# Linear attention and MLP on one core: scores and states per 64 tokens from block 1 on, with another order of the work

## The chip, the core and the metric

The kernel runs on one core of one Trainium2 chip. A core has TensorE (PE, matrix products; its weight loads are listed apart as PEld), VectorE (DVE), ScalarE (ACT), GpSimd (POOL) and SyncE (SP), which here only issues transfers. The engines run side by side and wait for one another through semaphores. On-chip memory is SBUF; PE writes into PSUM, which has eight banks. The metric is device time in microseconds (us), lower is better.

## What is computed

Inputs are x (4, 8, 768, 32), decays a (4, 8, 768), B and C (4, 8, 768, 16), and an MLP with g_ln (256), w_ch1 (256 x 1024) and w_ch2 (1024 x 256), all float32. Cut to what matters:

```python
# per batch and head; chunk = 32, state starts at 0
cum = np.cumsum(np.log(np.clip(a, 1e-06, 1.0)), axis=-1)          # within the chunk
M = einsum('in,jn->ij', C, B) * exp(cum_i - cum_j) * causal
y[chunk] = M @ x + (C @ state) * exp(cum_i)
state = exp(cum_last) * state + sum_j exp(cum_last - cum_j) * B_j x_j
# then per token, over the 8 x 32 = 256 features of all heads:
xn = (y - mean(y)) / sqrt(var(y) + 1e-06) * g_ln
out = y + relu(xn @ w_ch1) @ w_ch2
```

The result does not depend on the chunk length except by rounding, so a kernel may carry the state over other stretches.

## The kernel before, in words

The 768 tokens are 6 blocks t of 128. Within a block, tokens are cut into halves of 64 (HALF, index j), the partitions 0 to 63 and 64 to 127 of a tile; the four batches are split in NU = 2 (u) by NV = 2 (v), and heads are paired (q, four pairs; g, two groups of four heads). The steps, by the name that the order at the end of the file gives them:

- Head: the constants (`ld early`, on the ACT queue) and the decays (`ld a`, SP) are loaded; logarithms (`l1`, `l2`), sums and their exponentials (`e`, `x`, `so`, `sm`, `mb`, `sp`, `em`) give decay tables; two scans on DVE (`u`, `d`) give the decays since the start of a sub-chunk of 32 and to its end. For block 0 a product spreads these over all rows (`U`, `ur`); for later blocks they go out to memory and come back broadcast (`ro`, `ld ud`).
- `C`, `cm`, `B`: scaled C (split by even and odd head) and scaled B. `ones`, `W`: the mask tiles WW (two, one for each u), filled with the causal mask and then, for each block, with decays (three copies for each u, line 162).
- `G t u` (line 381): scores of one u, 128 tokens against 128. Keys of the first half meet all 128 queries (256 columns), keys of the second half only theirs (128 columns). `R t u q` (line 388, DVE): scores times mask.
- `I t` (line 400): queries of 128 tokens times the carried state; `V t u` (line 415): R times x, added in the same PSUM tile; `Z t` (line 427): what the block adds to the state, in a third part of the same PSUM tiles. `K`, `S`, `sb` (lines 432, 441, 445): the old state decayed, the new state, and its copy with a head mask, which I of the next block reads. So the state is carried once per 128 tokens, and Z of a block stands behind its I.
- The weights come in as 64-bit words and are put together (`k0`, `k2`, `k3`, `kr`, `f`), centred (`gd`, `wc`, `wm`, `ws`) and split in an upper and a lower part (`wh`, `wl`).
- The MLP: `y`, `yh`, `yl` copy and split y; `T`, `tw`, `tc` turn it to token order through memory; `st`, `ag`, `rs`, `rc` are its statistics. `h t m` (line 510): six products for one eighth of the hidden layer, in block 0 for each u apart (256 columns), later for all 512; `hh` (ACT) and `hl` (DVE) empty its bank. `o t b` (lines 537, 538) is the output of one batch, `oe` adds the residual, `od` stores it.

The order is written out in one string (ISSUE) of such names with an engine letter; each engine works through its own instructions in that order, and the transfers of SP are one queue in that order too. PSUM is one pool of eight banks, each taken by one tile at a time. `fill` products keep PE busy at the start. A product of float32 operands is two matmuls in the trace, one of float32r operands is one.

## Time and profile before

| | before |
|---|---|
| median of 3 runs | 190.06 us (190.02 to 193.27) |
| the profiled execution | 190.03 us |
| its span, first to last instruction | 188.3 us |
| PE busy | 181.6 us (96%), 2440 matmuls |
| DVE, ACT, POOL busy | 134.5, 72.9, 51.6 us |
| mean granted TensorE clock | 0.997 of full speed |

Busy time is the time in which at least one instruction of the engine runs. A row of the timeline is: start, time, engine, line, operation, out<-in, count, and in brackets the idle time of the engine just before it and what ended that. Matmuls overlap, so what one costs is read from the start of a group to the start of the next. A q behind an engine's name (SPq) means its sequencer.

### The profile page before, as it was taken

Reading aid. Unit: us, or ns where it says so; the run is one execution under the profiler, and the core shown is the slowest. Engines: PE = TensorE matmul, PEld = TensorE weight load, DVE = VectorE, ACT = ScalarE, POOL = GpSimd, SP = SyncE. Lnnn points to the kernel's source line nnn. Section 1 sums busy time; section 2 is a strip of 40 time slices with the busy share of each in tenths; the row PEclk is TensorE's granted clock in tenths of the full one; section 3 lists DMA queues with packets and bytes.
Section 4 is the critical chain, followed back from the end, with each engine's and each line's share of the span. In section 5 each row is a group of like instructions: output and inputs, shape, how many; then the busy total and the mean of one; then the engine's idle time right before and its main releaser. Section 6 shows DMA issues by size and latency. Waiting matters only on the chain.

```text
span 188.3 us, 5714 instructions
## 1 busy us (share of the span) xinstructions
PE 181.6 (96%) x2440; PEld 148.6 (79%) x2440; DVE 134.5 (71%) x302; ACT 72.9 (39%) x148; POOL 51.6 (27%) x65
## 2 busy tenths in 40 slices
PE   8979999999999999999998999999999999999992
PEld 8655589987878778788776887888888888888892
DVE  4899999998986797776984846659607574545841
ACT  7799999719434124421341201233102330034100
POOL 3162646624978941230032530000002000000000
PEclk9999999999999999999999999999999999999998
DMA  5999993843883913572150000363001035100102
GB/s 188 410 370 251 334 376 139 216 136 93 292 285 97 215 42 139 173 252 88 44 151 7 3 0 28 109 193 91 3 0 56 31 141 139 35 20 3 56 28 84
DMA packets 16729, 25.04 MB, mean 133 GB/s; under 512 B 4160, under 2 KB 10688, under 8 KB 16704
## 3 DMA queue, kind: packets, MB, share of 16 engines
q1 hardware_dynamic: 16560, 24.45, 40.3%
q8 instruction: 19, 0.31, 0.7%
q10 hardware_dynamic: 144, 0.23, 0.3%
q14 instruction: 6, 0.05, 0.1%
HBM read 18.06 MB, written 6.62 MB: 131 GB/s over the span
## 4 chain that ended last, share of the span: by engine, by line
PE 92%; ACT 4%; DVE 1%; issue 1%
PE ph L510 37%; PE po L537 23%; PE po L538 12%; PE yps L415 6%; PE G L381 4%; PE idle L556 2%; PE yps L427 2%; PE yps L400 2%; DVE R L388 1%; PE wc L226 1%; PE po L534 1%; ACT WW L162 1%; PE wc L227 1%; ACT raw L207 1%; ACT yh L162 1%
## 5 line engine op out<-in xcount | busy, mean ns | idle before, releaser
L537 PE MATMUL po<-w,hh 128*128 128x512 f32 x184 | 64.9, 396 | 0.1
L516 ACT ACTIVATE hh<-ph 128x512 fp32r<-128x512 f32 (+1 forms) x56 | 28.3, 536 | 74.0 <-PE ph L510 48.9
L510 PE MATMUL ph<-yh,w 128*128 128x512 f32 (+1 forms) x224 | 54.6, 365 | 0.0
L538 PE MATMUL po<-w,hl 128*128 128x256 f32 x184 | 47.9, 281 | 0.0
L522 DVE SCALAR_TENSOR_TENSOR hl<-ph,hh 128x512 fp32r<-128x512 f32 (+1 forms) x56 | 32.2, 604 | 17.1 <-ACT hh L516 17.1
L510 PEld LDWEIGHTS ph<-yh,w 128*128 128x128 f32 x224 | 38.2, 189 | 7.1 <-issue 0.3
L537 PEld LDWEIGHTS po<-w,hh 128*128 128x128 f32 x184 | 33.7, 188 | 7.1 <-ACT y L162 0.4
L538 PEld LDWEIGHTS po<-w,hl 128*128 128x128 f32 x184 | 34.7, 188 | 1.7
L510 PE MATMUL ph<-yl,w 128*128 128x512 f32 (+1 forms) x112 | 31.2, 360 | 0.0
L388 DVE TENSOR_TENSOR R<-G,WW 128x384 f32<-128x384 f32 x48 | 24.6, 546 | 5.6 <-PE G L381 4.9
L547 DVE SCALAR_TENSOR_TENSOR o<-po,rstd,ytok 128x256 f32<-128x256 f32 x24 | 11.5, 477 | 21.2 <-PE po L537 19.1
L510 PEld LDWEIGHTS ph<-yl,w 128*128 128x128 f32 x112 | 20.0, 189 | 3.5
L162 POOL COPY WW<-wt 32x512 f32<-32x512 f32 (+1 forms) x15 | 10.4, 695 | 17.0 <-DVE R L388 16.4
L162 POOL CAST yh<-y 128x512 fp32r<-128x512 f32 x5 | 3.3, 676 | 40.9 <-PE ph L510 33.5
L381 PE MATMUL G<-cm,bs 32*64 32x256 f32 (+1 forms) x384 | 12.0, 335 | 1.7 <-DVE bs L351 1.0
L162 ACT COPY WW<-wt 32x512 f32<-32x512 f32 (+1 forms) x21 | 12.8, 614 | 0.9 <-DVE rstd L501 0.7
L381 PEld LDWEIGHTS G<-cm,bs 32*64 32x64 f32 x384 | 7.4, 131 | 6.0 <-issue 2.4
L212 POOL TENSOR_TENSOR top<-top,raw 128x512 int32<-128x512 int32 x6 | 8.1, 1361 | 14.3 <-ACT WW L162 4.5
L547 DVE SCALAR_TENSOR_TENSOR o<-po,rstd,o 128x256 f32<-128x256 f32 x23 | 11.1, 484 | 0.8
L415 PEld LDWEIGHTS yps<-R,xt 64*32 64x32 f32 x768 | 10.1, 105 | 2.0 <-issue 1.2
L415 PE MATMUL yps<-R,xt 64*32 64x64 f32 (+1 forms) x768 | 11.2, 249 | 0.0
L490 DVE BATCH_NORM_STATS2 st<-ytok 128x6 f32<-128x256 f32 x24 | 9.4, 415 | 0.0
(100 smaller groups left out, 178.2 us busy)
## 6 DMA issues: line engine op xcount, KB each, us to landing
raw<-in_w_dram SPq DMA_DIRECT2D x8, 512.0 KB, 6.1
xt<-in_x_dram SPq DMA_DIRECT2D x6, 512.0 KB, 6.0
scr<-yx SPq DMA_DIRECT2D x6, 512.0 KB, 2.9
ytok<-scr SPq DMA_DIRECT2D x24, 128.0 KB, 3.0
out_dram<-o SPq DMA_DIRECT2D x24, 128.0 KB, 1.7
ud<-scr SPq DMA_DIRECT2D x10, 256.0 KB, 4.0
c<-in_cn_dram SPq DMA_DIRECT2D x6, 256.0 KB, 4.7
b<-in_bn_dram SPq DMA_DIRECT2D x6, 256.0 KB, 3.9
```

Source lines behind the costliest of these rows:

```text
L162: (e.copy if e is nc.scalar else e.tensor_copy)(dst, src)
L212: e.tensor_tensor(out=f, in0=f, in1=words.pop((w, *at))[0], op=ALU.add)
L381: nc.tensor.matmul(G[q][HALF * v:HALF * (v + 1), :, at], bs[r, i0 + HALF * j:i0 + HALF * (j + 1)], cm[r, :, i0 + HALF * j:i0 + P], start=T ...
L388: nc.vector.tensor_tensor(out=flat(R), in0=flat(tiles.pop(("G", t, u, q))), in1=flat(WW[u][:, 2 * q:2 * q + 2]), op=ALU.mult)
L415: nc.tensor.matmul(tiles["y", t, v, g][c:c + 32, u, HALF * j:], x[p, (j * NU + u) * NH + h], tiles["R", t, u, h // 2][p, h % 2, at], start ...
L490: nc.vector.bn_stats(out=st, in_=tiles["ytok", t][:, :, b])
L510: nc.tensor.matmul(ph, W1[m // 4, k][:, s, mc], v[:, k, tok], start=(i == 0), stop=(i == len(cmb) - 1))
L516: nc.scalar.activation(tiles["hh", t, m][:, tok], tiles["ph", t, m, u], AF.Relu)
L522: nc.vector.scalar_tensor_tensor(out=tiles["hl", t, m][:, tok], in0=tiles.pop(("ph", t, m, u)), scalar=0.0, in1=tiles["hh", t, m][:, tok]. ...
L537: both = lambda: nc.tensor.matmul(po, hh, w[:, :, at], start=(m == 0), stop=last, skip_group_check=True)
L538: low = lambda: nc.tensor.matmul(po[:, 0], hl, w[:, 0, at], start=False, stop=False, skip_group_check=True)
L547: nc.vector.scalar_tensor_tensor(out=parts(o), in0=parts(po[:, i]), scalar=tiles["rstd", t][:, b], in1=rest, op0=ALU.mult, op1=ALU.add)
```

## The change

- From block 1 on the scores of a block are two squares of 64 by 64 tokens instead of the triangle of 128: `G t` is one step for both u, every product has 128 columns, and its result is one full bank for each q. The masks for it are one tile WC, filled by `on` (two copies of the causal mask) and `W t` (two copies per block). `R t q` is then four products of 512 columns instead of eight of 384. Block 0 stays as it was.
- The state is carried per 64 tokens: `I t` reads the state before the block for the first half and the state in its middle for the second half, 64 columns each; `Z t` stands ahead of it, has two banks of its own and is kept apart by half; `K t j`, `S t j` and `sb t j` are done for both halves. Block 5 now needs Z for its first half.
- `V t` has two parts by head group g instead of by u, all products with 64 columns, and the parts may stand apart.
- The sums and tables have seven coefficient blocks instead of six and `rg` builds four row groups, so that `ur` is four products of 128 columns instead of one of 512.
- Some constants share buffers (early, ends, own_ini), the pool of R has 8 buffers instead of 12, and the last block's bt is half loaded.
- The order (ISSUE) is new throughout. On SP, a and the first w1 piece are followed by the other three w1 pieces, then by the late constants, c and b.

Core of the diff, without the tables and the order:

```diff
-    def score(t, u):
+    def score(t, u=None):
 
         bs, cm = tiles["bs", t], tiles["cm", t]
+        if t:
+            G = [banks.tile([P, NU, 2, P], F32, tag="bank", name=f"G{t}{q}") for q in range(NQ)]
+            for j in range(2):
+                for u in range(NU):
+                    for q in range(NQ):
+                        r = slice(2 * DS * q, 2 * DS * (q + 1))
+                        for v in range(NV):
+                            at = slice((v * NU + u) * P + HALF * j, (v * NU + u) * P + HALF * (j + 1))
+                            nc.tensor.matmul(G[q][HALF * v:HALF * (v + 1), u, :, HALF * j:HALF * (j + 1)], bs[r, at], cm[r, :, at], start=True, stop=True)
+            for q in range(NQ):
+                tiles["G", t, q] = G[q]
+            return
...
-                    nc.tensor.matmul(tiles["y", t, v, q // 2][f, u], tiles["sbd", t - 1][r, b], c2[r, b * P:(b + 1) * P], start=(u == 0), stop=False, skip_group_check=True)
+        summed(t)
+        for j in range(2):
+            state = tiles["sbd", t, 0] if j else tiles["sbd", t - 1, 1]
...
+                        nc.tensor.matmul(tiles["y", t, v, q // 2][f, u, HALF * j:HALF * (j + 1)], state[r, b], c2[r, b * P + HALF * j:b * P + HALF * (j + 1)],
+                                         start=(u == j == 0), stop=False, skip_group_check=True)
...
-        Z = tiles["Z", t] = [tiles["y", t, v, 0][:, NU] for v in range(NV)]
+        Z = tiles["Z", t] = [banks.tile([P, 2, P], F32, tag="bank", name=f"Z{t}{v}") for v in range(NV)]
         for u in range(NU):
-            for j in range(2):
+            for j in range(1 if t == NT - 1 else 2):
...
-    def kept(t, e=nc.vector):
-        S = tiles["K", t] = p1.tile([P, NB, 2 * HD], F32, tag="K", name=f"K{t}")
-        e.tensor_tensor(out=S, in0=tiles["S", t - 1], in1=emt[:, t].unsqueeze(2).to_broadcast([P, NB, 2 * HD]), op=ALU.mult)
+    def kept(t, j, e=nc.vector):
+        K = tiles["K", t, j] = p1.tile([P, NB, 2 * HD], F32, tag="K", name=f"K{t}{j}")
+        e.tensor_tensor(out=K, in0=tiles["S", t, 0] if j else tiles["S", t - 1, 1], in1=emt[:, t, j].unsqueeze(2).to_broadcast([P, NB, 2 * HD]), op=ALU.mult)
```

What this does to the order on the engines, at three places. First PE, the scores of block 1, before (G are the four score tiles, ph a hidden tile of block 0, emps the spread of the decays):

```order
L510 MATMUL ph_503<-yl_394,w_287 128x256
L381 MATMUL G_517<-cm_478,bs_501 64x2x128 x2
L381 MATMUL G_518<-cm_478,bs_501 64x2x128 x2
L381 MATMUL G_519<-cm_478,bs_501 64x2x128 x2
L381 MATMUL G_520<-cm_478,bs_501 64x2x128 x2
L381 MATMUL G_517<-cm_478,bs_501 64x2x64 x2
L381 MATMUL G_518<-cm_478,bs_501 64x2x64 x2
L381 MATMUL G_519<-cm_478,bs_501 64x2x64 x2
L381 MATMUL G_520<-cm_478,bs_501 64x2x64 x2
L296 MATMUL emps<-mblk,cst 128x120
L510 MATMUL ph_546<-yh_393,w_396 128x256
```

and with the change (the last of its four rounds of G, and the first rows of Z, the block's addition to the state):

```order
L409 MATMUL G_544<-cm_501,bs_526 64x2x64 x2
L409 MATMUL G_545<-cm_501,bs_526 64x2x64 x2
L409 MATMUL G_546<-cm_501,bs_526 64x2x64 x2
L409 MATMUL G_547<-cm_501,bs_526 64x2x64 x2
L483 MATMUL Z_592<-xt_585,be_358 32x64
L483 MATMUL Z_593<-xt_585,be_358 32x64
```

One u with wide and narrow products became four equal rounds for both u, and Z follows at once, where before the hidden layer went on.

Second PE, where I of block 1 meets V, before:

```order
L400 MATMUL yps_775<-c_763,sbd_733 64x128
L400 MATMUL yps_777<-c_763,sbd_733 64x128
L415 MATMUL yps_774<-R_702,xt_499 32x128
L415 MATMUL yps_776<-R_702,xt_499 32x128
L415 MATMUL yps_774<-R_702,xt_499 32x128
```

and with the change:

```order
L451 MATMUL yps_718<-c_689,sbd_699 64x64
L451 MATMUL yps_720<-c_689,sbd_699 64x64
L468 MATMUL yps_717<-R_583,xt_585 32x64
L468 MATMUL yps_719<-R_583,xt_585 32x64
L468 MATMUL yps_717<-R_583,xt_585 32x64
```

I and V stand as before, with 64 columns each; sbd_699 is the state in the middle of block 1.

Third ACT, from its start (WW and WC are mask tiles, cst constants and logarithms, cfr coefficients, top and raw weight words, wt decays), before:

```order
L162 COPY WW_89<-causal 128x1536
L162 CAST cfr<-cst 128x384
L263 ACTIVATE cst<-cst 128x192
L162 COPY uds<-uds 128x160
L193 ACTIVATE top_142<-raw_137 128x512
L277 ACTIVATE wt<-ew 128x384
L207 ACTIVATE raw_137<-raw_137 128x512
```

and with the change:

```order
L169 COPY WC<-early 128x1024 x2
L169 COPY WW_88<-early 128x1536
L273 ACTIVATE cst<-cst 128x192
L203 ACTIVATE top_132<-raw_130 128x512
L169 CAST cfr<-cst 128x448
L217 ACTIVATE raw_130<-raw_130 128x512
L169 COPY uds<-uds 128x160
```

Two more mask copies stand ahead of the logarithm (cst<-cst), and weight work stands ahead of the coefficients and of the scan's copy (uds).

## Rows read from the trace of the kernel before

**Rows 1.** The page's first part: busy time, share of the span and instructions

```profile
PE 181.6 (96%) x2440; PEld 148.6 (79%) x2440; DVE 134.5 (71%) x302; ACT 72.9 (39%) x148; POOL 51.6 (27%) x65
```

**Rows 2.** Timeline of PE, block 2's scores and block 1's addition to the state

```profile
45.27 0.91 PE L381 MATMUL G<-cm,bs 32*64 32x256 f32 x32
46.10 0.86 PE L427 MATMUL yps<-xt,be 64*32 64x64 f32 x64
46.96 0.50 PE L537 MATMUL po<-w,hh 128*128 128x512 f32 x1
47.29 0.28 PE L538 MATMUL po<-w,hl 128*128 128x256 f32 x1
47.41 0.39 PE L537 MATMUL po<-w,hh 128*128 128x512 f32 x1
47.65 0.28 PE L538 MATMUL po<-w,hl 128*128 128x256 f32 x1
```

**Rows 3.** Timeline of PE, I and V of block 1

```profile
39.90 0.70 PE L400 MATMUL yps<-c,sbd 32*64 32x128 f32 x32
40.54 1.82 PE L415 MATMUL yps<-R,xt 64*32 64x128 f32 x128
42.29 0.50 PE L537 MATMUL po<-w,hh 128*128 128x512 f32 x1
```

**Rows 4.** Timeline of PE's weight loads (PEld), V of block 1

```profile
40.54 1.66 PEld L415 LDWEIGHTS yps<-R,xt 64*32 64x32 f32 x128 [0.17 <-issue]
```

**Rows 5.** Timeline of PE, block 4: I, and G interrupted

```profile
98.19 0.69 PE L400 MATMUL yps<-c,sbd 32*64 32x128 f32 x32
...
100.42 0.65 PE L381 MATMUL G<-cm,bs 32*64 32x256 f32 x4
101.81 0.90 PE L381 MATMUL G<-cm,bs 32*64 32x256 f32 x28 [0.74 <-issue]
```

**Rows 6.** The chain that ended last: start, us, what; hidden products

```profile
31.04 5.95 PE ph L510 x48
...
117.25 12.48 PE ph L510 x54
```

**Rows 7.** Timeline of all engines at the start: ACT's idle time

```profile
2.16 1.47 ACT L162 COPY WW<-causal 128x1536 f32<-128x1536 f32 x1
...
3.91 0.51 ACT L162 CAST cfr<-cst 128x384 f32<-128x384 uint8 x1 [0.28 <-DMA cst<-in_consts_dram]
...
...
5.04 0.33 ACT L162 COPY uds<-uds 128x160 f32<-128x160 f32 x1 [0.35 <-DVE uds L308]
...
6.61 0.49 ACT L277 ACTIVATE wt<-ew 128x384 f32<-128x384 f32 x1 [0.67 <-PE ew L274]
...
9.44 3.66 ACT L162 COPY WW<-wt 32x512 f32<-32x512 f32 x6
...
19.17 0.37 ACT L162 CAST yh<-yps 128x256 fp32r<-128x256 f32 x1
```

**Rows 8.** Timeline of PE: Z of block 0, the first hidden product, the spread

```profile
21.47 1.12 PE L427 MATMUL yps<-xt,be 64*32 64x64 f32 x64 [0.25 <-ACT yh L162]
22.52 0.74 PE L510 MATMUL ph<-yh,w 128*128 128x256 f32 x4
...
26.70 0.45 PE L296 MATMUL emps<-mblk,cst 32*128 32x120 f32 x2
```

**Rows 9.** The page's fifth part: what empties a hidden tile

```profile
L516 ACT ACTIVATE hh<-ph 128x512 fp32r<-128x512 f32 (+1 forms) x56 | 28.3, 536 | 74.0 <-PE ph L510 48.9
...
L522 DVE SCALAR_TENSOR_TENSOR hl<-ph,hh 128x512 fp32r<-128x512 f32 (+1 forms) x56 | 32.2, 604 | 17.1 <-ACT hh L516 17.1
```

**Rows 10.** Instructions on tile S: duration ns min/median/max, first and last start

```profile
L441 DVE TENSOR_TENSOR S<-yps,K x8: 254/281/291, 47.5 to 105.1; 128x128 f32<-128x128 f32 x8
L445 POOL TENSOR_TENSOR sbd<-S,cst x4: 633/637/642, 36.4 to 109.4; 128x256 f32<-128x256 f32 x4
```

**Rows 11.** Stretches: us, each engine's busy time, PEclk, DMA share, GB/s

```profile
4.00:5.00 1.00, 1.00 (x6) 1.00 (x6) 0.89 (x3) 0.69 (x2) 0.00 (x0) 1.00 1.02 399
```

## The prediction, made before the change was run

> **What bounds the kernel now.** I read the page's busy times first: TensorE is busy 181.6 of 188.3 us, every other engine far less [rows 1]. A busy TensorE need not be at its peak, so the next view is its timeline, read from the start of one group to the start of the next. An MLP output tile alternates a 512-column and a 256-column product, 0.24 us and 0.12 us apart [rows 2]; the hidden products run at 5.95/48 = 0.124 us (256 columns) and 12.48/54 = 0.231 us (512 columns) [rows 6]. These paces hold from the first hidden product at 22.52 us [rows 8] to the end: 16 half tiles x 6 x 0.124, 40 full tiles x 6 x 0.231, 23 output tiles x 8 x 0.36 and some 3 us for the last one make about 137 us, the attention groups of blocks 1 to 5 (below) about 27, and 22.5 + 137 + 27 is 186.5 of 188.3. So there is almost no slack behind 22.5 us. The change is worth what it takes out of TensorE's own sequence, plus what it does to the first 22.5 us.

> **Prices.** The trace counts two matmuls for each fp32 product, and so do I. One G group (16 of 256 and 16 of 128 columns) takes 45.27 to 46.10, 0.83 us; one Z (64 of 64 columns) 46.10 to 46.96, 0.86 [rows 2]; one I (32 of 128) 39.90 to 40.54, 0.64; one V (64 of 128 and 64 of 64) 40.54 to 42.29, 1.75 [rows 3]. Each holds the pause in which the next weights wait for the old group to leave, 0.17 us [rows 4]. Without it: G 0.66 us, which is 13.8 ns per 128 columns; I 0.47/32 = 14.7 ns per 128; Z 0.69/64 = 10.8 ns at 64 columns; V 1.58/128 = 12.3 ns on average, just what 13.8 and 10.8 give. So 128 columns are paid by the column, and halving them saves only a quarter. Returning to the MLP costs the first output product 0.33 instead of 0.24 [rows 2]; I take the same for entering, 0.2 us per excursion.

> **The sum, part by part** (blocks 1 to 5 unless said; start against start).
> 1. *Scores.* Two G groups (1.66 us) become one of 64 matmuls with 128 columns: 64 x 13.8 to 14.7 ns + 0.17 = 1.05 to 1.11, taken as 1.08. Five blocks: **-2.9** (-3.05 to -2.75).
> 2. *State products I.* 32 of 128 columns become 64 of 64. The trace has none of 64 columns in this tile shape. Lower bound: columns alone, no change. Upper: I's own price per matmul, 64 x 14.7 + 0.17 = 1.11 us, +2.35 in all. Nearest is Z, equal in columns: 64 x 10.8 + 0.17 = 0.86, **+1.1**.
> 3. *Values V.* Now 128 matmuls of 64 columns, the very form of Z: 128 x 10.8 + 0.17 = 1.55, **-1.0**. Bounds: V's own mean, 0; columns alone, -3.5, which Z's row excludes, so -1.3 at 10.2 ns.
> 4. *V in two places.* Blocks 1 to 4 split V in halves, before only block 4: three more pauses, **+0.5**. In return G lies in one place and beside Z: 13 excursions instead of 15, **-0.4**.
> 5. *Carry.* Block 5 now has half a Z, 32 x 10.8 ns: **+0.35**. The others keep their 64.
> 6. *A stall.* In block 4, TensorE stood still for 0.74 us inside a G group, waiting for nothing that the profile shows, after I, V and Z had passed 160 matmuls from 98.19 to 100.42, 2.2 us [rows 5]. That place no longer exists in this form. I take **-0.74**; a new one would give it back (bound 0).
> 7. *Head.* ACT is the engine to watch: before the first yh at 19.17 it has idled only 0.28 + 0.35 + 0.67 = 1.3 us after 2.16 [rows 7]. It gains two mask copies of 1024 columns (1.47 x 1024/1536 = 0.98 each) and loses one gd copy to POOL (0.4); W for block 1 is two copies of 1024 for three of 512 at 0.61 (+0.3): +1.9 less the 1.3 idle is 0.6 us, so yh at 19.8. From yh to the first hidden product were 3.35 us, 1.05 of them Z of block 0 [rows 8], which now stands behind that product: 19.8 + 2.3 = 22.1, and 23.15 with Z paid, against 22.52; the spread of the decays (emps), before paid later among the products, is now paid here, some 0.4 back. Net **+0.2**. Bounds: -0.5 if ACT's idle absorbs more, +2 if the logarithm, now behind three mask copies instead of one, is late for everything. On SP, four w1 transfers of 0.5 MB now go ahead of c and b: 2.8 MB to c's end, at the 399 GB/s of that stretch [rows 11] 7 us of transfer, so c is there between 9 and 10 us. DVE has eleven instructions between its first scan and its first use of c, and I take these to last longer; uncovered, the difference goes into the +2. The scans' input and the constants were already the first transfers of their queues, so that part gives nothing.
> 8. *Off the path.* R is 4 instead of 8 products per block on DVE, W two copies instead of six: less work for engines that TensorE rarely waits for, counted as nothing. Their cover is TensorE's own 96%. The second K, S and sbd per block go to DVE and POOL; see the third rival.

> Sum: -2.9 + 1.1 - 1.0 + 0.5 - 0.4 + 0.35 - 0.74 + 0.2 = -2.9 us. The profiled execution took 190.03 us (188.3 of span, 1.7 around it), the median of the runs is 190.06. Forecast: **187.1 us**. With the bounds of 1 to 7 taken together the ends are 185.8 and about 192.

> [...] The 0.74 us came after the densest stretch of instructions in the run [rows 5]; by rows alone it goes or it comes back. [...]

> **The rivals.**
> - *A price per matmul, not per column.* If I keeps 14.7 ns, V 12.3 and G 0.66/32 = 20.6 ns each whatever the width, I gives +2.35, V 0, G 64 x 20.6 + 0.17 = 1.49 or -0.85, and with the rest the sum is +1.2: 191.3 us, slower than before. Against it: I and G have the same tile shape and differ by their columns, 14.7 to 20.6 ns. Chance 0.06. [...]
> - *PSUM.* Z had a corner of the y tiles; now it holds two of eight banks from G's end until both S are formed, while G holds four. The MLP then has two, and a bank comes back only after hh (0.54) and hl (0.60) [rows 9]. One such wait of about 0.6 us per block is +3.0: 190.1 us. For it: four banks of G go together with two of Z; against: G's banks return with each R, and before, TensorE waited for no bank at all. Chance 0.20.
> - *The state chain, slower than before.* I of a block now needs the state in the middle of the same block: S twice 0.28, sbd 0.64 on POOL, then the second K, S and sbd [rows 10]: with K like sbd, 0.56 + 0.64 + 0.56 + 0.64 = 2.4 us and more, with a weight product on POOL in its way in block 1. Cover between Z and I: seven half tiles, 7 x 0.74 = 5.2 us, in block 1; three full ones, 3 x 1.39 = 4.2, in block 2 [rows 6]; 8 us and more later. From 2.9 us of waits on (both early blocks late by 1.5) it is slower than before; 2% slower needs 6.7, a chain of about 7 us twice. Chance 0.08, most of it near 191.
> - *More than forecast.* I and V at 10 ns and a head without loss: 185.3. Chance 0.06.
> - The forecast: 0.60.

> **How the numbers follow.** The forecast's own range is 185.8 to 188.6. Two per cent, about what a measurement of this kernel can tell from no change, is 186.26 and 193.9. Nearly a third of the forecast's 0.60 lies under 186.26, and all of the rival that gains more: 0.25 faster. Over 193.9 lie the far ends of the first and third rivals: 0.05. The rest, 0.70, is within 2%. The range 185.3 to 190.4 leaves out the price per matmul, the far end of the chain and a tenth of the others.

> **What would show it.** G once per block, about 1.08 us from start to start; I 0.86; V halves 0.86 each; the first hidden product near 22; no PE idle over 0.3 us except at the head. Wrong would be: I over 1.1, idle before I released by sbd or S, waits of ph or po for a bank, or yh later than 21.

## The result, and the profile after

The changed kernel takes 193.88 us in the median of 20 runs (191.22 to 197.45), the kernel before 190.68 in 20 runs beside it. The ratio is 1.0105, with an interval of 1.0068 to 1.0143: about 1% slower, within 2%, and above the upper end of the range. Ratios compare undisturbed runs; medians are of all runs.

| | before | after |
|---|---|---|
| profiled execution, its span | 190.03, 188.3 us | 191.44, 189.7 us |
| PE busy | 181.6 us, x2440 | 179.8 us, x2648 |
| DVE, ACT, POOL busy | 134.5, 72.9, 51.6 us | 128.7, 74.3, 56.7 us |
| mean granted clock | 0.997 | 0.991 |

The first part of the page of after, to lay beside [rows 1]:

```profile
PE 179.8 (95%) x2648; PEld 150.5 (79%) x2648; DVE 128.7 (68%) x292; ACT 74.3 (39%) x144; POOL 56.7 (30%) x64
```

TensorE is busy 1.8 us less, with 208 matmuls more, and still the kernel ends later. First the part that behaves as forecast, PE's timeline of after in block 1 (compare [rows 2, 3]):

```profile
30.17 1.21 PE L409 MATMUL G<-cm,bs 32*64 32x128 f32 x64
31.31 0.86 PE L483 MATMUL Z<-xt,be 64*32 64x64 f32 x64
...
60.91 0.91 PE L451 MATMUL yps<-c,sbd 32*64 32x64 f32 x64
61.75 0.86 PE L468 MATMUL yps<-R,xt 64*32 64x64 f32 x64
62.54 1.40 PE L566 MATMUL ph<-yh,w 128*128 128x512 f32 x4
```

The last three rows are block 2's. From start to start G takes 1.14 us, I 0.84 (in block 1 alone 0.98), one half of V 0.79. Behind the head no wait of PE names a bank, S or sbd. The head is another matter; PE's timeline of after from 5.7 to 27.8 us:

```profile
5.76 0.55 PE L297 MATMUL msps<-cst 128*32 128x8 f32 x12 [0.76 <-ACT cst L273]
6.76 0.74 PE L284 MATMUL ew<-cst,cfr 128*64 128x96 f32 x16 [0.46 <-ACT cfr L169]
8.47 1.78 PE L350 MATMUL rows<-own_ini,rg 128*128 128x128 f32 x8 [0.96 <-DVE own_ini L343]
...
14.56 1.62 PE L420 MATMUL G<-cm,bs 32*64 32x256 f32 x64 [0.87 <-ACT early L230]
...
24.02 0.74 PE L566 MATMUL ph<-yh,w 128*128 128x256 f32 x4
...
24.93 0.76 PE L483 MATMUL Z<-xt,be 64*32 64x64 f32 x53
26.84 0.33 PE L483 MATMUL Z<-xt,be 64*32 64x64 f32 x11 [1.16 <-issue]
27.10 0.74 PE L566 MATMUL ph<-yh,w 128*128 128x256 f32 x4
```

The first hidden product starts at 24.02 (before 22.52, with Z already paid [rows 8]), and Z of block 0 stands still for 1.16 us in its middle, released by "issue", that is, by nothing that the profile shows. All such waits of PE in after, in the list of waits (total, times, longest):

```profile
PE Z L483 <- issue: 1.2, 1, 1.2
...
PE G L409 <- issue: 0.7, 1, 0.7
PE po L593 <- issue: 0.5, 1, 0.5
PE yps L468 <- issue: 0.2, 1, 0.2
```

I split both runs at the start of the second hidden tile and at the start of the last product. Between them I count as stalls the steps from one instruction to the next at the places that the section on the stalls finds, each less 0.13 us for the usual pace:

| us | second hidden tile | last product | stalls between | rest |
|---|---|---|---|---|
| before | 23.54 | 184.70 | 1.0 | 160.2 |
| after | 27.10 | 186.18 | 2.2 | 156.9 |

The rest is 3.3 us shorter; 0.37 of that is emps, the spread of the decays, which after pays ahead. So the steady work gains 2.9 us, the stalls behind the head take 1.2 back, and the head takes 3.56: the stall of 1.16, emps 0.37 and 2.0 us of lateness.

### The profile page after: what moved, and what is told of

The parts are those of the page before. It is cut to its first block, busy times and chain, and to the rows that moved or that the text cites. A ratio compares the mean times of both kernels' runs of the same rounds, so it can differ in the third digit from the quotient of the medians.

```text
span 189.7 us, 6134 instructions
## 1 busy us (share of the span) xinstructions
PE 179.8 (95%) x2648; PEld 150.5 (79%) x2648; DVE 128.7 (68%) x292; ACT 74.3 (39%) x144; POOL 56.7 (30%) x64
## 4 chain that ended last, share of the span: by engine, by line
PE 91%; ACT 4%; issue 3%; DVE 1%
PE ph L566 36%; PE po L593 23%; PE po L594 12%; PE yps L468 4%; PE G L409 3%; PE Z L483 2%; PE yps L451 2%; ACT WW L169 1%; PE wc L236 1%; PE wm L242 1%; PE po L590 1%; ACT WC L169 1%; PE yps L471 1%; PE rows L350 1%; PE wc L237 1%
## 5 line engine op out<-in xcount | busy, mean ns | idle before, releaser
L578 DVE SCALAR_TENSOR_TENSOR hl<-ph,hh 128x512 fp32r<-128x512 f32 (+1 forms) x56 | 32.7, 605 | 19.8 <-ACT hh L572 19.7
L522 POOL TENSOR_TENSOR yl<-y,yh 128x512 fp32r<-128x512 f32 x6 | 8.3, 1377 | 38.0 <-DVE yh L169 36.7
L429 DVE TENSOR_TENSOR R<-G,WC 128x512 f32<-128x512 f32 x20 | 12.9, 676 | 3.6 <-PE G L409 1.9
L169 ACT COPY WC<-wt 32x1024 f32<-32x1024 f32 x8 | 8.3, 1038 | 7.8 <-DVE R L429 7.7
L169 ACT COPY y<-yps 128x256 f32<-128x256 f32 x14 | 5.2, 380 | 10.2 <-PE yps L468 9.1
L468 PE MATMUL yps<-R,xt 64*32 64x64 f32 x640 | 8.5, 224 | 0.2 <-issue 0.2
L468 PEld LDWEIGHTS yps<-R,xt 64*32 64x32 f32 x640 | 6.9, 105 | 1.8 <-issue 1.3
L488 POOL TENSOR_TENSOR K<-S,emt 128x256 f32<-128x256 f32 x7 | 4.7, 676 | 12.1 <-DVE S L497 12.1
L530 DVE STREAM_TRANSPOSE yx<-y 128x512 f32<-128x512 f32 x12 | 8.2, 694 | 0.1
L409 PE MATMUL G<-cm,bs 32*64 32x128 f32 x320 | 6.8, 279 | 0.8 <-issue 0.7
```

The lines of the kernel that those rows point to most:

```text
L169: (e.copy if e is nc.scalar else e.tensor_copy)(dst, src)
L409: nc.tensor.matmul(G[q][HALF * v:HALF * (v + 1), u, :, HALF * j:HALF * (j + 1)], bs[r, at], cm[r, :, at], start=True, stop=True)
L429: nc.vector.tensor_tensor(out=R.rearrange("p (u k) -> p u k", u=NU), in0=tiles.pop(("G", t, q)).rearrange("p u i k -> p u (i k)"), in1=WC[ ...
L468: nc.tensor.matmul(tiles["y", t, v, g][c:c + 32, u, HALF * j:HALF * (j + 1)], key, tiles["R", t, h // 2][p, u, h % 2, HALF * j:HALF * (j + ...
L522: e.tensor_tensor(out=tiles["yl", t][:, :, tok], in0=tiles["y32", t][:, :, tok], in1=tiles["yh", t][:, :, tok].bitcast(F32), op=ALU.subtract)
L578: nc.vector.scalar_tensor_tensor(out=tiles["hl", t, m][:, tok], in0=tiles.pop(("ph", t, m, u)), scalar=0.0, in1=tiles["hh", t, m][:, tok]. ...
```

## The experiments

**Theory.** Two things eat the gain: the head's new order (late transfers, mask copies, a slowed clip, an idle TensorE whose clock falls), and stalls that the fetch of instructions causes where short matmuls stand densely. **Rivals:** the matmuls cost more than forecast (already against the rows above); one single cause in the head explains it; the stalls are waits for data or banks that the trace mislabels.

### One cause of the head at a time: e1, e2, e3, e4

The edits move names in the order (e4 is all three together):

```diff
 e1
-ld:s late, fill 9, ... fill 10, fill 11, ld:s c 0, cm 0 0, fill 12
+ld:s w1 1 0, fill 9, fill 10, fill 11, fill 12, ur 0
 e2
-on:a 0, ld:s a, on:a 1, ...
+... kr 2 0, on:a 0, on:a 1, W:a 1
 e3
-dd:a 0, rg:p, U:v 1
+iv, rg:v, ... dd:a 0, U:v 1
```

> The changed kernel with the four zero products 9 to 12 moved back to a place ahead of ur 1's companion ur 0, where nothing waits behind them. Theory that they are a cause of the late head: they stand in front of the second product of rows (12.64 us in the profile after) and TensorE idles ahead of them, so rows comes some 1.5 us earlier, the granted clock from 8 to 14 us is higher than the 0.69 and 0.50 seen after, and the time falls by 1.0 to 1.5 us. Rival, that VectorE's scan and ScalarE's logarithm bound the head whatever TensorE does there: yh stays within 0.3 us of 21.58, time within 0.3 us.

> The changed kernel with ScalarE's two copies of the chunk masks (1.99 us) moved from in front of the logarithm to just before the weights W of block 1. Theory that they hold up the head: the logarithm starts near 4.3 us instead of 5.35, as before, and yh comes 0.5 to 1.0 us earlier than 21.58; time down by as much. Rival, that the transfer of the scans' input or VectorE sets the time of the first scan anyway: logarithm earlier, yh within 0.3 us, and the copies now delay yh instead, so no gain or 0.5 us lost.

> The changed kernel with the instruction rg given from GpSimd back to VectorE, behind iv. Theory that VectorE's clip took 1.10 us instead of 0.25 because a GpSimd operation ran beside it: clip back at 0.25 us, first scan near 4.5 us instead of 5.28, yh 0.5 us or more earlier, time down by about 0.5. Rival, that clip waits for something else or that the masks on ScalarE come last anyway: clip still near 1 us, or clip 0.25 and yh unchanged within 0.3 us.

> All three moves together. If the head's loss of 2.25 us over before is made of these three: yh at 19.3 to 20.0, first hidden product at 22 to 22.6 us, granted clock 1.0 through the head, time about 2 us under the changed kernel's (near 189.5 in the profiled execution), the stalls inside the attention groups unchanged (about 1.2 us in Z of block 0 and 1.4 us behind it). If the head is bound elsewhere: less than 1 us.

Medians 197.3, 193.24, 193.41 and 193.22 us; ratios 1.0231 [1.0128, 1.0334], 1.0172 [1.0099, 1.0244], 1.0103 [1.0038, 1.0167], 1.0162 [1.0123, 1.0202]. None gained clearly on the 1.0105 of after. The profiled execution of e1 ran at a mean granted clock of 0.658, so its length says nothing; its G came 0.25 us earlier all the same, and what the fills cost at full clock stays open.

The part that each edit aimed at did move. In after, DVE's clip of the decays (ends<-a) takes 1.10 us while POOL builds rg; before, the same size took 0.25, and in e3, with rg on DVE, 0.25 again. Timelines of ACT, DVE and POOL in after, and last of DVE in e3:

```profile
5.35 0.36 ACT L273 ACTIVATE cst<-cst 128x192 f32<-128x192 f32 x1
...
4.07 1.10 DVE L319 TENSOR_SCALAR ends<-a 128x186 f32<-128x186 f32 x1
...
3.95 1.11 POOL L338 TENSOR_TENSOR rg<-cst 128x512 f32<-128x512 f32 x1 [1.62 <-DMA cst<-in_consts_dram]
...
3.97 0.25 DVE L319 TENSOR_SCALAR ends<-a 128x186 f32<-128x186 f32 x1
```

In after the clip ends 0.11 us behind rg, at 5.17 and 5.06 us; why it takes longer beside rg no run shows.

The logarithm (cst<-cst) came at 5.35 behind three mask copies; in e2 it came at 4.09, but then the moved copies delay yh, in e2's timeline of PE, and likewise in e4's, here with its timeline of DVE:

```profile
25.20 0.62 PE L566 MATMUL ph<-yh,w 128*128 128x256 f32 x3 [0.65 <-ACT yh L169]
```

```profile
13.69 1.63 PE L420 MATMUL G<-cm,bs 32*64 32x256 f32 x64 [2.97 <-DVE bs L371]
...
24.15 0.62 PE L566 MATMUL ph<-yh,w 128*128 128x256 f32 x3 [0.54 <-ACT yh L169]
...
9.78 0.76 DVE L207 TENSOR_SCALAR top<-top 128x512 int32<-128x512 int32 x2 [1.39 <-ACT top L203]
...
11.49 1.41 DVE L361 SCALAR_TENSOR_TENSOR cm<-c,cst,rows 128x512 f32<-128x512 f32 x2 [0.35 <-DMA c<-in_cn_dram]
```

With all three, TensorE is ready almost 3 us ahead of bs, because DVE's cm, which stands before bs, starts at 11.49 only: it stands behind the unpacking of weights, which itself waited 1.39 us for ACT, and then waits 0.35 us more for the transfer of c. The first hidden product of e4 comes at 23.23, 0.8 us before that of after, but behind it come the wait for yh, a granted clock of 0.50 from 25.7 to 29.1 us, and stalls of 3.0 us instead of 2.2. So none of these three carries it alone: when one goes, the next is as late.

### The transfers: e5, e6, and e10 on the kernel before

In after, c is issued behind four weight pieces and lands 7.4 us later (SP's timeline, then the transfers of 3 to 14 us):

```profile
3.73 0.84 SPq L153 DMA_DIRECT2D c<-in_cn_dram  x1
```

```profile
c<-in_cn_dram SPq DMA_DIRECT2D x1, 256.0 KB, 7.4
```

That is about 11.2 us, not 9 to 10. DVE itself was busy until 10.87 there and started cm at 11.26, so in after c held cm up by 0.4 us at most. e5 puts the late constants, c and b among the weight pieces of e4 and has cm and B ahead of the unpacking; e6 also spreads the mask copies, moves the second scan forward and W of block 1 and two fills back; e10 does the reverse to the kernel before, the four pieces ahead of c and b.

```diff
 e5
-ld:s w1 0 1, ... ld:s w1 1 1, ld:s w1 0 0, ... ld:s late, ... ld:s c 0, ... ld:s b 0
+ld:s w1 0 1, ld:s late, ld:s c 0, ... ld:s w1 1 1, ld:s b 0, ld:s w1 0 0, ... ld:s w1 1 0
 e6 (beside e5)
+l2, on:a 0, ... iv, d, dd:v 1, U:v 1, U:v 0, rg:v, ... dd:a 0, on:a 1
-on:a 0, on:a 1, W:a 1
+y:a 0 1 0, W:a 1
 e10
+ld:s w1 0 1, ld:s w1 1 1, ld:s w1 0 0, ld:s w1 1 0, ld:s late, ld:s c 0, ld:s b 0
```

> The kernel of the run with all three moves, and with the transfers of c, b and the late constants put right behind the first of the four w1 transfers (as before the change) instead of behind all four, their users cm and bs moved ahead of the unpacking that then waits longer. There G of block 0 stood 2.97 us for bs, and cm for the transfer of c. Theory that the transfers' order is the main cause of the late head: cm starts by 9.5 us instead of 11.49, G of block 0 by 11.7 instead of 13.69, and with it wc and V 2 us earlier (V near 17.1); yh gains less, about 1 us, since ScalarE has the mask copies in front of it there. Time 0.5 to 1.5 us under that kernel's 193.2. Rival, that the unpacking of w1 (now later) takes the place of c: G earlier, wc and V not, time unchanged or worse.

> As the run before, with the mask copies on ScalarE in the pauses in which it waited for w1, W of block 1 behind the first y copies, and VectorE's second scan and own columns ahead of rg. Theory that transfers, masks, rg and fills together are the whole loss of the head: yh at 18.7 to 19.7 us, first hidden product at 21.3 to 22.3, no granted clock under 1.0 in the head, and a profiled time of about 188.7 to 189.7 us: 2.2 us less at the head than the changed kernel, the stalls inside the groups of blocks 0 to 4 (2.5 us in all) as they are. Rival: the head is bound by the unpacking of w1 to the product wc, then yh stays above 20.5 and the time above 190.5.

> The kernel before with one thing of the change: all four w1 transfers ahead of the late constants, c and b, in the changed kernel's order. Theory: the transfers' order by itself makes the head late; cm waits for the transfer of c until 11 us or later (7.66 before), G of block 0 starts at 13 or later (10.10 before), the first hidden product comes 2 us or more later than 22.52, time up by 1.5 to 3.5 us. Rival, that c is not what the head waits for: first hidden product within 0.5 us, time the same.

Medians 195.32, 195.14, 196.54; ratios 1.0157 [1.0081, 1.0234], 1.0264 [1.0237, 1.029], and 1.032 [1.0288, 1.0353] for e10. PE in e5:

```profile
11.23 1.63 PE L420 MATMUL G<-cm,bs 32*64 32x256 f32 x64 [0.63 <-DVE bs L371]
...
15.33 2.04 PE L236 MATMUL wc<-top,early 128*128 128x512 f32 x2 [2.46 <-DVE R L434]
```

G comes 2.5 us earlier than in e4, and the centring products wc then wait 2.46 us for R, which stands on DVE behind the unpacking of weights that was put off. In e6 wc waits as long for the unpacking on ACT, the first hidden product comes at 25.91, and the forecast (188.7 to 189.7) is missed by far. In the kernel before, the early weight pieces alone are bad (timelines of DVE and PE in e10, then a window: us, busy PE, PEld, DVE, ACT, POOL, granted clock, DMA share, GB/s):

```profile
10.23 1.41 DVE L341 SCALAR_TENSOR_TENSOR cm<-c,cst,rows 128x512 f32<-128x512 f32 x2 [3.09 <-DMA c<-in_cn_dram]
...
12.63 1.59 PE L381 MATMUL G<-cm,bs 32*64 32x256 f32 x32 [4.02 <-DVE bs L351]
...
28.22 0.74 PE L510 MATMUL ph<-yh,w 128*128 128x256 f32 x4
```

```profile
12.00:14.00 2.00, 1.37 (x32) 0.88 (x32) 1.78 (x3) 1.95 (x4) 0.68 (x1) 0.50 1.09 384
```

The first hidden product comes 5.7 us later than in before. So in the kernel before the order of the transfers is enough to lose the head; in the changed kernel, putting it back did not win it (e5, e6). After TensorE had idled 4.02 us its granted clock stood at 0.50, and the centring products took 5.8 us instead of 3.6.

### The old head on the new kernel: e9, e12, e13, e14

e9 gives after the kernel before's order up to the first hidden product, e12 adds five fill products, puts bs right behind cm, with its transfer earlier, and splits the mask copies; e13 has W of block 1 on POOL, e14 prepares the first column's weights earlier.

```diff
 e12 (beside e9)
+gd:a 1, on:a 0, ... ur 0, ld:s w1 0 0, ld:s b 0, ... fill 11, fill 13, fill 14, fill 15, fill 16, fill 17, cm 0 1, B:v 0
 e13 (beside e12)
-y:a 0 1 0, W:a 1
+B:p 1, W:p 1
+V 0 1, f:p 1 1 1, mb:p
 e14 (beside e13)
+R 0 1 0, wl:v 1 0 1, wh:v 1 0 0, wl:v 1 0 0, ... V 0 1, fill 18, fill 19, fill 20, ... h 0 1 0, wm 1, sp, em
```

> The changed kernel with everything ahead of the first yh in the order that the kernel before has (transfers: w1 0 1, late constants, c, w1 0 0, b, w2 0, and then the other two w1; the unpacking of column 0 of w1 first; rg on VectorE; mask copies where before copied W of block 1, W of block 1 behind the y copies). Theory that the loss at the head is the order of the transfers and of the steps that follow them: cm by 8.5 us, G of block 0 by 11, wc by 14.5, yh by 19.8, the first hidden product by 22.8 us, and the time 1 to 2.5 us under the changed kernel's, near 189.5 to 190.5 in the profile (stalls at the places 193 past a multiple of 256 as far as the blocks fall on groups). Rival, that the changed computation itself (rows as 16 products, masks, gd on GpSimd) makes the head late: yh stays above 20.8, time within 0.7 us of the changed kernel's.

> The run with the old head order, in which TensorE idled 1.7 us ahead of G of block 0 and its clock was then granted at 0.50 for the products wc (6.0 us instead of 3.6), with five more zero products in that gap, bs right behind cm, and the mask copies in two pauses of ScalarE. Theory: the granted clock then stays at 1.0 through the head, G of block 0 starts at 10.2 us or earlier, wc takes 3.6 us, the first hidden product comes at 22.0 to 22.8, as before the change or earlier, and with the stalls left as they are (2.5 to 4 us in all) the time is 187.8 to 189.5 us, 0.5 to 1.3 per cent under the kernel before, with little spread. Rival, that the clock or the unpacking keeps the head late however it is ordered: first hidden product after 23.5, time above 190.5.

> The kernel of the twelfth run with W of block 1 on GpSimd, which idles 3.9 us there, instead of on ScalarE ahead of cm of block 1; and the unpacking step on GpSimd ahead of be of block 0. Theory that the changed computation is 2.5 us faster and only head and stalls took it: G of block 1 no longer waits (1.1 us before), the clock stays at 1.0 behind it, first hidden product at 21.9 to 22.5, and the time is 188.3 to 190.0 us, at or under the kernel before (190.3), with 2.5 to 4 us of instruction stalls still in it. Rival, that the steady part has another cost: time above 190.7 with G of block 1 on time.

> The kernel of the thirteenth run, in which the first hidden product waited 1.5 us for the lower part of its weights (behind the unpacking of column 1 of w1 on VectorE) and the clock fell after it. Here the weights of column 0 are finished first, three zero products fill TensorE's pause, and the products wm and emps stand behind the first hidden product. Theory: first hidden product by 21.5 us, no granted clock under 1.0 up to 34 us, and the time 1.5 to 2.5 us lower, 189.0 to 190.5, with the stalls at 193 past a multiple of 256 as they were (about 4 us in all). Rival, that another wait comes up behind it (wm or Z late): time above 191.

e9: 193.53 us (189.41 to 195.1; the lowest, at a mean clock of 1.000, is below the median of before, the others, at 0.982 to 0.991, above). Its profiled execution, 0.982, in PE's timeline and in windows:

```profile
10.59 1.00 PE L420 MATMUL G<-cm,bs 32*64 32x256 f32 x32 [1.69 <-DVE bs L371]
```

```profile
12.00:14.00 2.00, 2.00 (x39) 1.24 (x35) 2.00 (x5) 1.69 (x4) 2.00 (x2) 0.63 1.10 358
14.00:18.00 4.00, 4.00 (x16) 2.10 (x16) 3.83 (x9) 2.79 (x5) 0.40 (x2) 0.50 0.60 154
```

G comes 4 us earlier than in after, but behind an idle time of 1.69 us the granted clock falls to 0.50 and stays there while the centring products run. e12, with fills in that gap, keeps 1.00 there and starts the centring products at 13.45 us instead of 14.61: 191.81, ratio 1.006 [1.0024, 1.0096]; PE:

```profile
22.38 1.00 PE L566 MATMUL ph<-yh,w 128*128 128x256 f32 x4 [0.28 <-DVE w L255]
...
28.88 1.38 PE L409 MATMUL G<-cm,bs 32*64 32x128 f32 x64 [1.10 <-issue]
```

The first hidden product is back at 22.38, and the next wait follows: G of block 1 ("issue" in the row, but ACT makes its cm from 28.07 on, behind 2.09 us of W). e13 moves W away: 192.47, 1.0097 [1.0059, 1.0135]; now the weight tile w is 1.49 us late and the clock is 0.50 from 24.3 to 27.7 us. e14: 194.39, 1.0192 [1.0143, 1.024]; the first product comes at 19.73, but behind it TensorE waits 1.09 us for yl and 0.95 for the operand of wm, and the clock falls in the same way, to 0.78 in the mean of 22 to 26 us and 0.79 of 26 to 30. None of the four reached the time forecast for it.

### The stalls: e7, e8, e11, e15, e17

The page of after lists a queue of its own for instructions (packets, MB, share):

```profile
q8 instruction: 21, 0.34, 0.7%
```

Each packet is 16 KB; after has 21 of them for 5343 instructions of TensorE (loads, matmuls, semaphores), before 19 for 4918, about one for 256. I numbered these instructions in order of start and looked, behind the first hidden product, for steps of 0.33 us or more from one start to the next (a mere change of groups takes up to 0.33). Worked out from the trace of after, for the six such places and two others; "stood" is that step, the last column the time since the packet began:

```
instruction   starts   256 instructions before it took   stood   fetch began before it
 705           26.84     6.16                             1.37    2.50
 961           31.49     4.65                             0.00    2.72
1473           41.50     3.55                             0.44    2.52
2241           63.44     2.52                             0.33    2.34
2497           66.99     3.55                             0.96    2.43
3009           82.76     6.05                             0.77    2.40
3265           86.69     3.94                             0.36    2.29
4801          136.00     6.42                             0.00    1.96
```

All are 193 + 256 k. So is 3521 of before, the stall of [rows 5], and so is in the other runs every step that is over 0.4 us longer than its usual pace and that no late datum explains. Over before, after and e2 to e18, an instruction that stood for over 0.4 us starts 2.2 to 3.0 us after its packet began. The packet began 0.1 to 2.3 us after the previous such place, and the 256 instructions between would have taken 1.5 to 3.5 us without the stall. At 26 to 34 and at 68 to 86 us the packet often began later, up to 5.9 us after that place, and stretches of up to 6.6 us stalled. Data transfers are often busy there (in after a share of 1.05 from 26 to 29 us and 0.92 from 75 to 80); that they hold the packet back is not shown. Not every dense block stalls: in before, 4289 came 1.87 us after 4033 without a stall, its packet having begun 0.88 us before that. These rows agree with a fetch of TensorE's instructions in blocks of 256, one 16 KB packet for each; that is my reading of them, and no row shows the fetch itself.

If that is so, instructions put in front move the places. e7 replaces 4 fills by 36 tiny zero products (4 instructions each), e8 6 fills by 62, e11 5 fills of the kernel before by 57 (the diff shows e7). Nothing reads these products. e17 (on e16, below) moves hidden and output products between the bursts; e15 does so on e14.

```diff
 e7, e8, e11
-fill 0, fill 1, fill 2, fill 3
+tiny 36
+def tiny(n): ... nc.tensor.matmul(spot[c:c + HD], zero[:HALF].to_broadcast([HALF, HD]), zero[:HALF].to_broadcast([HALF, 2 * HD]), ...)
 e17 (beside e16)
-G 1, R 1 2 ... Z 1, S 1 0, h 0 3 0
+G 1, h 0 3 0, h 0 4 1, ... Z 1
+I 2, h 1 0, ... V 2 1, h 1 6, ... G 3, h 1 1, ... Z 3, h 1 5, ... I 3, h 2 4, ... G 4, o 1 2
```

> The changed kernel with 36 small products of zeros in place of four of the zero products at the very start (about the same time on TensorE, nothing reads them): every later instruction of TensorE stands 128 places further on, nothing else changes. The stalls of the changed kernel (1.16 us in Z of block 0, 0.69 in G of block 3, 0.49 in an output tile, with two of 0.1 to 0.2) come at instructions 705, 1473, 2497, 3009 and 3265 of TensorE, all 193 more than a multiple of 256. Theory that they are the fetch of instructions in blocks of 256: they move by half a block, to other places, and by my estimate from the spacing of the instructions are worse there, 4 to 7 us in all instead of 2.7, the largest in groups of many short products; time up by 2 to 4 us. Rival, that these groups stall by themselves (a semaphore, a bank, the shape): stalls at the same places and of the same size, time unchanged within 0.5.

> The same with 62 small products in place of six: a shift of 224 places. Theory of the fetch: the stalls nearly go, 0.7 us or less left in all, time down by 1.2 to 2 us, with G, Z, I and V at the same prices otherwise. Rival: same stalls in the same groups, time unchanged.

> The kernel before with 57 small products of zeros in place of five of the first zero products: every later instruction of TensorE moves by 208 places, nothing else. Theory of the fetch in blocks of 256: the stall of 0.74 us in G of block 4 goes and others come at 193 past a multiple of 256, near 59 us (1.2 to 1.7), 102 us (about 1.4) and 132 us (about 1.7), time up by 2.5 to 4 us. Rival, that before was free of stalls by its shorter groups: no new stall above 0.3 us, time within 0.5.

> The same with the order of TensorE's groups alone changed: two half tiles between G and Z of block 1, the two V halves of blocks 1 and 2 apart from I and from each other, a hidden tile between V and G and between G and Z of block 3, an output tile between G and Z of block 4. No instruction is added or taken away, so every boundary of 256 falls on the same instruction number, but fewer short matmuls lie between two of them. Theory of the fetch: of the 4 us of stalls some 3 go, five more excursions cost about 0.25 us each, so the time falls by 1.5 to 2.2 us against the run beside it, to 187.2 to 188.8, below the kernel before by 1 per cent or more. Rival, that the stalls come from something in the groups themselves: same stalls, time unchanged or 1 us up by the excursions.

> The same kernel with only the order of TensorE's groups changed: two half tiles between G and Z of block 1, V's second half of block 1 two half tiles later, a hidden tile between I and V and between V's halves of block 2, one between G and Z of block 3 and one behind Z, one between I and V of block 3, an output tile between G and Z of block 4. Theory of the fetch: stalls fall from 3 to 4.5 us to 0.5 to 1.5 in all; five more excursions cost about 0.25 us each; time 1 to 2.5 us under the run beside it, 187.2 to 189.0, under the kernel before by 0.7 to 1.6 per cent. Rival, that the stalls belong to the groups: same stalls, time as beside it or up to 1.2 us longer.

e7: 194.77, ratio 1.0222 [1.0182, 1.0262], stalls behind the head 5.7 us instead of 2.2, at 961, 2753, 3521 and 4801, and one more ahead of it, at 705; Z of block 0 runs through. Two of them in its timeline of PE, in groups that ran through in after:

```profile
68.39 0.30 PE L483 MATMUL Z<-xt,be 64*32 64x64 f32 x3 [1.19 <-issue]
...
88.39 0.33 PE L483 MATMUL Z<-xt,be 64*32 64x64 f32 x11 [1.19 <-issue]
```

e8: 191.98, 1.0084 [1.0045, 1.0123], stalls 3.1 at 961, 1217, 1729, 2753 and 4033: the places moved as expected, but the size, 0.7 or less, was missed. e11: 196.55, 1.0306 [1.0258, 1.0353]; the stall at 3521 is gone and five others came, 5.2 us in all (the head, too, is 1.7 us later than in before), the largest:

```profile
61.91 0.33 PE L415 MATMUL yps<-R,xt 64*32 64x64 f32 x11 [1.29 <-issue]
```

No datum and no bank has changed in these three, so the third rival falls: these waits go by the count of instructions. The first rival falls by the rows of G, I and V. The second falls for the causes of e1 to e4, as far as four runs each can tell; that the order of the transfers is the root of the rest is neither shown nor excluded by e5, e6 and e10.

Spreading the bursts does take the stalls away, but costs as much: e17 has 0.74 us of them against 3.0 in e16, yet 193.06 us against 191.36, ratio 1.0156 [1.0119, 1.0193]. From the first output product to the last product it took 142.99, e16 142.07, with 1.0 us less of stalls, so 1.9 us went elsewhere. I of block 3 is 0.7 of it, 1.57 us instead of 0.84, with waits for its data inside; the other 1.2 go to the four more changes between attention and hidden or output products in that stretch, by my estimate 0.3 us each. (e15: 196.64, 1.0271; it copies part of y of block 1 before one part of V is added, its clock was 0.50 from 23.6 to 33.9 us, and it settles nothing.)

### Toward a better head: e16 and e18

```diff
 e16 (beside e12)
-y:a 0 1 0, W:a 1
+B:p 1, W:p 1
+e w, fill 18, fill 19, ... f:p 1 1 1, wl:v 1 0 1
 e18 (beside e16)
-B:p 1, W:p 1
+y:a 0 0 0, W:a 1 0, ... y:a 0 1 0, W:a 1 1
```

> The head of the twelfth run, with W of block 1 on GpSimd (there it made G of block 1 wait 1.1 us), the lower weights of column 0 and the y parts ahead of the unpacking of w2 on VectorE, and two more zero products in a pause of TensorE (8 instructions). Theory: first hidden product at 21.9 to 22.4 us, no wait in front of it, granted clock 1.0 from 22 to 34 us, stalls of 3 to 4.5 us at 193 past a multiple of 256, time 189.3 to 190.8. Rival, another late step in the head: time above 191.

> The kernel of the sixteenth run with the two copies W of block 1 on ScalarE, one in each of two pauses (1.0 and 1.3 us long there) ahead of cm of block 1, instead of on GpSimd. Theory: VectorE's instructions beside them are back at 0.68 us, Z of block 1 does not wait (1.64 us before), the clock stays at 1.0 from 30 to 34 us, first hidden product at 22.5 or earlier, stalls of 3 to 4 us at 193 past a multiple of 256 remain; time 188.8 to 190.2 us, between 0.8 per cent under the kernel before and equal to it. Rival, that the banks or another engine hold block 1 back anyway: time 190.5 or more.

e16: 191.36, 1.0059 [1.0028, 1.0089]. Its timeline shows why W does not belong on POOL: beside its copies two of DVE's weight operations take 1.52 us each instead of 0.68, and Z waits for a bank that hl empties late. The last row is e18's, in which no POOL copy runs beside the same operation.

```profile
28.76 1.52 DVE L212 SCALAR_TENSOR_TENSOR top<-raw,top 128x512 int32<-128x512 int32 x1
...
27.01 2.73 POOL L169 COPY WC<-wt 32x1024 f32<-32x1024 f32 x2
...
30.67 1.50 PE L483 MATMUL Z<-xt,be 64*32 64x64 f32 x64 [1.64 <-DVE hl L578]
...
27.36 0.68 DVE L212 SCALAR_TENSOR_TENSOR top<-raw,top 128x512 int32<-128x512 int32 x1
```

e18 puts the two copies of W into two pauses of ACT. Profiled execution 189.47 us (span 187.8, clock 1.000), and on PE:

```profile
22.02 0.75 PE L566 MATMUL ph<-yh,w 128*128 128x256 f32 x4
...
29.72 0.73 PE L483 MATMUL Z<-xt,be 64*32 64x64 f32 x49 [0.50 <-issue]
...
40.30 0.66 PE L468 MATMUL yps<-R,xt 64*32 64x64 f32 x41 [0.90 <-issue]
```

Its account: second hidden tile 23.72, last product 184.18, stalls 3.2, rest 157.2. With a head as early as that of before, the gain of the computation appears: the rest is 3.0 us shorter than before (0.37 of it is emps), and 2.2 of that goes into stalls. The ratio is 0.9928 [0.9887, 0.9969], from four of its twelve runs (188.91 to 189.47 us, clock 0.998 to 1.000); the other eight took 191.8 to 198.0 at a mean clock of 0.981 to 0.991. The median of all is 193.69 against 190.47, no better than the 193.88 of after. So this kernel is the shortest of the three only where its clock holds, which it mostly did not.

## Why the prediction was wrong, step by step

- *1, scores.* Forecast 1.08 us for G, measured 1.14, a little over the bounds of 1.05 to 1.11: -2.6 instead of -2.9. Right in kind.
- *2, I.* Forecast 0.86, measured 0.84 (0.98 in block 1). Right, and the price per matmul falls with it: that rival wanted 1.11 for I and 1.49 for G. Its terms as listed add up to +1.4, not +1.2, and so to 191.4 us; that the profiled execution took just this is chance.
- *3 and 4, V and its halves.* Halves forecast at 0.86, measured 0.79, V of block 5 in one piece 1.42: together about -1.0 instead of -0.5. Z, beside G, takes 0.79 instead of 0.86, as the -0.4 for fewer excursions had it. With the half Z of step 5 the steady work gained 2.9 us where steps 1 to 5 had 2.35.
- *6, a stall.* The failed step. "That place no longer exists" treated as a property of one group what goes by the count of instructions (in most of the stretches that stalled, 256 of them would have passed in 1.5 to 3.5 us). The change adds 208 matmuls, 416 instructions with their loads, and sets G beside Z and I beside V. Forecast -0.74, bound 0; measured 1.16 in block 0's Z and 2.2 behind it, against 1.0 before: +2.4. The bound of nothing excluded a loss without a reason, although [rows 5] had a stall of 0.74 us behind 160 matmuls in 2.2 us.
- *7, the head.* Mis-sized as well: forecast +0.2, bounds -0.5 to +2; without the stall and emps +2.0, at the bound that I had named but not chosen. c was to land between 9 and 10 us and landed near 11.2, yh was to come at 19.8 and came at 21.58. The late logarithm and DVE's queue were seen; the clip beside rg and TensorE's clock were not. In after's windows the clock falls behind the waits of 0.76, 0.46 and 0.96 us that end between 5.7 and 8.5 us:

```profile
6.00:8.00 2.00, 1.05 (x26) 0.86 (x23) 1.78 (x6) 2.00 (x6) 0.00 (x0) 1.00 0.95 320
8.00:10.00 2.00, 1.53 (x8) 1.52 (x8) 1.41 (x5) 1.56 (x5) 0.00 (x0) 0.69 0.99 378
10.00:12.00 2.00, 2.00 (x18) 1.59 (x17) 1.61 (x4) 1.44 (x5) 0.64 (x2) 0.50 1.05 416
```

- *8, off the path.* Right.
- *The ends of the range.* The bounds of 1 to 7, simply added, give 184.9 and about 192; the 185.8 does not follow that way. The upper end would have held 191.44, though not by its own terms: step 6 alone went 2.4 past its bound.
- *Rivals.* PSUM, the one with the largest chance, did not come: after has no wait for a bank (e16 has one, by its own edit). Nor did the state chain.

The misses are 3.1 (step 6), 1.8 (step 7) and -0.55 (steps 1 to 5), 4.4 in all: 187.1 + 4.4 is 191.5, and the profiled execution took 191.44. As these terms divide up that same execution, the sum must close; it is no separate proof. What else supports the division is that stalls move with the count (e7, e8, e11), and that with an early head (e18) the profiled execution took 189.47.

Open: the median of after lies 2.4 us above its profiled execution. All nine runs of over 194 us have a mean clock of 0.962 to 0.982, and where it fell in them no profile shows. Nor is the clock all of it: runs of after took 193.4 at 0.997 and 193.9 at 1.000, but also 191.98 at 1.000. Open too: how the 2.0 us of the head divide among their causes, since each alone gave nothing; and why one kernel's clock falls in some executions and not in others.

## What to carry to other kernels

Count instructions as well as columns: a change that cuts the same work into shorter matmuls should be held against the pace at which instructions arrive (here, by my estimate from the stalls above, about 256 in 3.5 us), and a stall that goes by the count of instructions cannot be argued away with its place. In a head where every engine is nearly full, price a new order by the landing time of each transfer and by what TensorE does while it waits, since behind idle time there the clock of what follows can also be lower (0.50 behind 1.69 us in e9, 1.00 with five fills in that gap in e12; but 1.00 up to 18 us behind 2.97 us in e4). A cause removed alone may show nothing, because another is nearly as late; take them together, and look each time at what became the last. And repeat the run: one early execution (e18) is not yet a faster kernel.
